# First block of a two-layer Hedgehog/Mish kernel: statistics behind the low weights, one fold chunk between a half's products, the second block's rows counted and normalized ahead of the second queries

## The chip, the cores and the metric

The kernel runs on one core of one Trainium2 chip. A core has five engines that each work through their own instructions in order: TensorE (PE in the profile; its weight loads are PEld), VectorE (DVE), ScalarE (ACT), GpSimd (POOL) and SyncE (SP), which issues the DMA transfers. They wait for each other through semaphores. The metric is the time of one execution on the device in microseconds (us).

## The reference

Two kinds of layer alternate, twice each, on x of 2048 rows by 640 columns, all in 32-bit floats:

```python
def _A_ref(x, wqkv, w_phi, wo):
    B, S, D = x.shape
    H = 32; Dh = D // H
    qkv = (lambda x, *d: x.transpose(*d))((x @ wqkv).reshape(B, S, 3, H, Dh), 2, 0, 3, 1, 4)
    q, k, v = qkv[0], qkv[1], qkv[2]
    pq = jnp.einsum("bhsd,hdf->bhsf", q, w_phi)
    pk = jnp.einsum("bhsd,hdf->bhsf", k, w_phi)
    phi_q = jnp.concatenate([_softmax(pq, axis=-1), _softmax(-pq, axis=-1)], axis=-1)
    phi_k = jnp.concatenate([_softmax(pk, axis=-1), _softmax(-pk, axis=-1)], axis=-1)
    kv = jnp.einsum("bhsf,bhsd->bhfd", phi_k, v)
    z  = jnp.einsum("bhsf->bhf", phi_k)
    num = jnp.einsum("bhqf,bhfd->bhqd", phi_q, kv)
    den = jnp.einsum("bhqf,bhf->bhq", phi_q, z)[..., None] + 1e-6
    o = num / den
    return (lambda x, *d: x.transpose(*d))(o, 0, 2, 1, 3).reshape(B, S, D) @ wo

# _B_ref: dense (w1, b1), Mish, dense (w2)
x = x + _A_ref(_layernorm(x, axis=-1), A_wqkv, A_w_phi, A_wo)
x = x + _B_ref(_layernorm(x, axis=-1), B_w1, B_b1, B_w2)
x = x + _A_ref(_layernorm(x, axis=-1), A_wqkv, A_w_phi, A_wo)
x = x + _B_ref(_layernorm(x, axis=-1), B_w1, B_b1, B_w2)
```

## The kernel before

The 2048 rows are worked in eight blocks of 256, each of two tiles of 128 rows (`NB`, `BT`). Each weight and each normalized, transposed activation is kept as a high part (a copy rounded to the matmul's input type, made on ACT) and a low part (what the rounding left, made on DVE or POOL). A product is then three matmuls: high by high, high activation by low weight, low activation by high weight (`project_half`).

The attention layer has a first half (`attend_first`), which makes the features of queries and keys and the values, sums keys by values into one PSUM bank (`kva`), and sends the query features to DRAM; and a second half (`attend_second`), which reads them back, averages and multiplies by `wo`. The dense layer follows (`dense`).

In the very first layer the query and key weights are first folded with `w_phi`: `fold` multiplies a raw chunk of the transposed weights by the block-diagonal `w_phi` (`bd`, of which `differences` takes one feature per head from the others). For the queries there are five row chunks k of 128 (`KD`) by six column chunks t; t = 0 to 2 make the first half of the query weights (c = 0), t = 3 to 5 the second (c = 1). Each half needs five PSUM banks (`banks_of_five`), one for each k. `query_parts` (L527) splits the folded weights into high (`r2h`) and low (`r2l`). The key weights are folded later in the same way (`fold_keys`, L589) into `r1h` and `r1l`, two banks to a chunk k. The value weights are loaded and split by the generator `v_weights` (L178), one chunk at each `next`: an issue on SP, a copy on ACT, a subtraction here on POOL.

The first block runs by hand: L508 to L622 stand under a manual schedule, in which PE, SP, ACT, DVE and POOL keep the order of the code among these instructions. In other parts of the program the build decides the order of ACT, DVE and POOL, and it may place instructions of those parts between those of the hand-written block; so it does with the DMA issues on SP, too: `spill_qk_weights` (L204) of later blocks, the mask (L626) and the bias (L987) land among the loads of the first. Transfers use eight semaphores in turn (an issue waits for the landing of the transfer eight before it).

The stages of the hand-written block, in the order of PE: 24 transposes of the identity whose result nobody reads (L511), the folds of t = 0 and 1, the transposes of the first tile's rows (`turn`), the folds of t = 2, the first half's fifteen products, the folds of t = 3 to 5, the transposes of the second tile's rows, the second half's fifteen products, the second tile's thirty products, the key folds 0 to 4, the values of both tiles, and then the transposes of the second block's rows and its keys.

`features` (L415) makes query and key features out of a tile's products, in steps that the caller spreads: copies (ACT), two reductions and two subtractions (DVE, one of them on POOL where `pool_sub` is set), the exponential (ACT), a sum and reciprocal (DVE) and a product (POOL).

PSUM tiles `one` are four banks, `mm` two double banks, each handed out again when its readers are done: so the values of tile 1 write the bank that key fold 3's low part has read, and key fold 4 the double bank that fold 0's low parts have read.

Of the kernel before, what the change touches and what calls it, by code (L numbers as in the profile page):

```python
# [10 lines left out]
AF = mybir.ActivationFunctionType  # L11
# [5 lines left out]
P = 128  # L17
# [5 lines left out]
KD = D // P  # L23
KF = F // P
BT = 2
# [4 lines left out]
HC = D // 2  # L30
DF = DH - 1
FC = H * DF // 2
# [5 lines left out]
SKEW = 2  # L38
V_ORDER = (0, 1, 4, 2, 3)
FOLD = (6, 6, 6, 6, 4, 4)  # L40
TURNS = 24
LAYERS = 2
LN_EPS = 1e-5
DEN_EPS = 1e-6
# [7 lines left out]
def kernel(  # L52
# [25 lines left out]
    def one_tile():  # L78
        return psum.tile([P, 512], F32, tag="one", name="one", bufs=4)
# [271 lines left out]
    def row_tile():  # L351
        return work.tile([P, D], F32, tag="xn", name="xn", bufs=4)

    def normed(b, xt):

        xn = [row_tile() for _ in range(BT)]
        for t in range(BT):
            act(xn[t], xt[:, t, :], AF.Identity,
                                 bias=stats[:, b, 1, t:t + 1], scale=stats[:, b, 0, t:t + 1])
        return Transposed(xn)  # L360

    def normalize(b, dst, src):
        for t in range(BT):
# [26 lines left out]
            project_half(ps[c], xts, t, ws, col, c, ks, w=w, final=ks[-1])  # L390
        return ps

    def project_half(ps, xts, t, ws, col, c, ks=range(KD), w=HC, final=KD - 1):
        sl = slice(t * P, (t + 1) * P)
        cs = slice(col + c * w, col + (c + 1) * w)
        for k in ks:
            h, l, wh, wl = xts.hs[k], xts.ls[k], ws[k][0][:, cs], ws[k][1][:, cs]
            for n, (a, r) in enumerate(((h, wh), (h, wl), (l, wh))):
                nc.tensor.matmul(ps[:, :w], a[:, sl], r, start=(k == 0 and n == 0),  # L399
                                 stop=(k == final and n == 2))  # L400

    def both(ps, w=HC):

# [44 lines left out]
    def attend_first(layer, x_src, first):  # L448
# [30 lines left out]

        def queries(xts, i, ps=None):  # L480
            e = query_tile(i)
            yield from features(project(xts, i % BT, q_ws, 0, w=FC) if ps is None else ps, e, True)

            nc.vector.transpose(e, e)  # L484
            b, t = divmod(i, BT)
            dst = e_d[b].rearrange("(j f) (t q s) -> t q f j s", f=32, t=BT, s=32)
            for q in range(4):
                nc.sync.dma_start(dst[t, q], e[32 * q:32 * q + 32].rearrange("f (j s) -> f j s", s=32))
                if b == NB - 1:
                    yield  # L490
# [15 lines left out]
        if first is None:  # L506
            E = mybir.EngineType
            with tc.manual_schedule(engines={E.PE, E.SP, E.Activation, E.DVE, E.Pool}):  # L508
                written[0] = True
                ps = one_tile()  # L510
                for _ in range(TURNS):  # L511
                    nc.tensor.transpose(ps[:, :P], ident, ident)
                xt = x_tile()
                rows = [row_tile() for _ in range(BT)]
                bd = big_tile()[:120, :720].rearrange("p (t c) -> p t c", t=6)

                def fetch_first(t):
                    nc.sync.dma_start(xt[:, t], row_block(x_src, 0)[:, t])

                def normalize_first(t):  # L520
                    act(rows[t], xt[:, t], AF.Identity, bias=stats[:, 0, 1, t:t + 1], scale=stats[:, 0, 0, t:t + 1])

                def banks_of_five():
                    ma, mb = mm_tile(), mm_tile()
                    return [ma[:, 0], ma[:, 1], mb[:, 0], mb[:, 1], one_tile()]

                def query_parts(banks, c, ks):  # L527
                    for n in range(2):
                        for k in ks:
                            fold_parts(q_ws, banks[k], k, c, (n,))  # L530

                fetch_first(0)
                load_phi(bd, False)
                raw = load_raw(0, range(3))
                load_phi(bd, True)
                fetch_first(1)
                raw += load_raw(0, range(3, 6))
                mvs = [norm_stats(0, xt)]
                differences(bd, 120, slice(0, 3), 120)
                norm_scale(0, mvs, 0)  # L540
                normalize_first(0)
                differences(bd, 120, slice(3, 5), 120)
                differences(bd, 80, slice(5, 6), 80)
                q_ws = [r2_pair(k) for k in range(KD)]
                kv_ws = [r1_pair(k) for k in range(KD)]
                xts = FirstRows()
                banks = banks_of_five()
                for t in range(2):
                    for k in range(KD):
                        fold(banks[k], bd, raw, k, t)  # L550
                turned, last = one_tile(), one_tile()
                xts.turn(0, rows[0], turned, last[:, :P])
                for k in range(KD):
                    fold(banks[k], bd, raw, k, 2)
                xts.split(0)
                query_parts(banks, 0, (0, 1))
                query_parts(banks, 0, (2, 3))
                query_parts(banks, 0, (4,))
                mvs = [norm_stats(1, xt)]
                norm_scale(0, mvs, 1)  # L560
                pq = [one_tile()]
                project_half(pq[0], xts, 0, q_ws, 0, 0, w=FC)
                vw = v_weights(kv_ws, nc.gpsimd)
                for _ in range(3):
                    next(vw)
                banks = banks_of_five()
                for k in range(KD):
                    for t in range(3, 6):
                        fold(banks[k], bd, raw, k, t)
                query_parts(banks, 1, (0, 1))  # L570
                normalize_first(1)
                query_parts(banks, 1, (2, 3))
                query_parts(banks, 1, (4,))
                xts.turn(1, rows[1], one_tile(), last[:, P:2 * P])
                xts.split(1)
                pq.append(one_tile())
                project_half(pq[1], xts, 0, q_ws, 0, 1, w=FC)
                next(vw)
                next(vw)
                raw = load_raw(1)  # L580
                g0 = queries(xts, 0, pq)
                next(g0)
                next(g0)
                p1 = project(xts, 1, q_ws, 0, w=FC)
                next(g0)
                g1 = queries(xts, 1, p1)
                next(g1)

                def fold_keys(k):  # L589
                    mm = None if k % 2 else mm_tile()  # L590
                    banks = [one_tile(), one_tile()] if k % 2 else [mm[:, 0], mm[:, 1]]
                    for t in range(6):
                        fold(banks[t // 3], bd, raw, k, t)
                    return lambda n: [fold_parts(kv_ws, banks[c], k, c, (n,)) for c in range(2)]

                parts = [fold_keys(k) for k in range(4)]
                parts[0](0)
                next(g1)
                parts[1](0)
                parts[0](1)  # L600
                next(g1)
                parts[1](1)
                parts[2](0)
                parts[3](0)
                next(g0)
                parts[2](1)
                parts[3](1)
                parts.append(fold_keys(4))
                parts[4](0)
                vs = [v_tile() for _ in range(BT)]  # L610
                xt = fetch(x_src, 1)
                mvs = [norm_stats(t, xt) for t in range(BT)]
                norm_scale(1, mvs)
                ready = last_scale[0]
                v = [values(xts, t, vs[t]) for t in range(BT)]
                next(v[0])
                next(g1)
                parts[4](1)
                nxt = normed(1, xt)
                kva = one_tile()  # L620
                nc.vector.memset(kva[:, :360], 0.0)
                next(v[1])  # L622
            written[0] = False
            with tc.manual_schedule(engines={E.PE, E.SP}):
                pending += [g0, g1]
                nc.sync.dma_start(mask, bass.AP(tensor=head_mask.tensor, offset=head_mask.offset,  # L626
                                                ap=[[1, 120], [21 * 120, 3], [1, 1]]))
                nxt.step()
                nxt.step()
                for t in range(BT):  # L630
                    g = keys(xts, t, vs[t])
                    next(g)
                    if t == 0:
                        nxt.step()
                    advance()
                    pending.append(g)
        else:
            nxt, kv_ws = first
            load_k_weights(kv_ws)
            q_ws = load_q_weights()  # L640
# [422 lines left out]
```

## Time and profile before

| | |
|---|---|
| median of 3 runs | 1363.98 us |
| lowest, highest | 1363.42, 1364.98 us |
| profiled execution, its own time | 1363.75 us |
| its span, first to last instruction | 1362.0 us |
| instructions | 30917 |
| bytes read from HBM, written | 104.61 MB, 62.59 MB |

The span is cut into 40 equal slices on the page; the first two of them, some 68 us, hold the work around the change. A digit is the busy share in tenths:

```profile
PE   9999999999999999999999999999999999999998
DVE  5988788877787887778778988878768776676775
DMA  9614324798614542334472434459974231233200
```

What is to be read there: PE is busy at nine tenths or more in nearly every slice; in the first slice the DMA engines are full and DVE is half idle, and in the second DVE is full. The rows of the timeline give start and duration in us, engine, line, operation, what is written from what, and in brackets the idle time before the instruction with what ended it.

### The profile page before, as it was taken

How to read it: one execution, taken by the hardware profiler on the slowest of the kernel's cores; microseconds unless marked ns; L12 is line 12 of the kernel's file. 1: busy time of each engine (PE TensorE's matmuls, PEld its weight loads, DVE VectorE, ACT ScalarE, POOL GpSimd, SP SyncE). 2: the span in 40 equal slices, each digit the busy share in tenths (PEclk: the TensorE clock that was granted, in tenths of full speed). 3: DMA queues.
4: the chain of work that ended last, by engine and by line, in shares of the span. 5: the costliest groups of instructions: out<-in, count | busy, mean ns of one | idle time of the engine just before them, and what ended most of it. 6: DMA issues, size and time to landing. Idle time of an engine off the chain costs nothing.

```text
span 1362.0 us, 30917 instructions
## 1 busy us (share of the span) xinstructions
PE 1349.2 (99%) x12890; PEld 1337.6 (98%) x12890; DVE 1063.8 (78%) x1805; ACT 584.5 (43%) x1039; POOL 471.0 (35%) x361
## 2 busy tenths in 40 slices
PE   9999999999999999999999999999999999999998
PEld 8999999999999999999999999989999999999998
DVE  5988788877787887778778988878768776676775
ACT  5443444322454545445444344432236444444443
POOL 3345644434222222222216556744341211111111
PEclk9999999999999999999999999999999999999999
DMA  9614324798614542334472434459974231233200
GB/s 343 175 41 76 80 41 86 224 283 304 190 39 96 117 117 72 61 101 111 135 241 56 82 71 78 79 144 278 278 256 130 78 79 30 88 97 98 76 22 20
DMA packets 350613, 169.21 MB, mean 124 GB/s; under 512 B 287225, under 2 KB 323817, under 8 KB 350473
## 3 DMA queue, kind: packets, MB, share of 16 engines
q1 hardware_dynamic: 350473, 167.23, 45.8%
q8 instruction: 101, 1.65, 0.5%
q14 instruction: 39, 0.32, 0.1%
HBM read 104.61 MB, written 62.59 MB: 123 GB/s over the span
## 4 chain that ended last, share of the span: by engine, by line
PE 93%; DMA 2%; DVE 2%; POOL 1%; ACT 0%; issue 0%; SPq 0%; DVEq 0%; POOLq 0%; ACTq 0%
PE mm L399 26%; PE one L859 25%; PE mm L901 24%; PE one L399 12%; PE mm L753 3%; PE one L311 2%; PE one L475 2%; DMA big<-e_d 1%; DMA v<-in_wv 1%; DVE r L484 0%; DVE r L438 0%; DMA big<-in_phi_bd 0%; POOL r L440 0%; POOL big L440 0%; DVE m L429 0%
## 5 line engine op out<-in xcount | busy, mean ns | idle before, releaser
L901 PE MATMUL mm<-r2h,ol 128*128 128x320 f32 x1280 | 304.9, 309 | 0.0
L885 POOL TENSOR_TENSOR ol<-big,ol 128x512 fp32r<-128x512 f32 (+1 forms) x98 | 129.4, 1321 | 486.8 <-ACT ol L884 402.8
L859 PE MATMUL one<-xtl,r1h 128*128 128x256 f32 x960 | 268.2, 279 | 0.0
L859 PE MATMUL one<-xth,r1l 128*128 128x256 f32 x960 | 268.0, 279 | 0.0
L859 PE MATMUL one<-xth,r1h 128*128 128x256 f32 x960 | 265.9, 279 | 0.0
L901 PEld LDWEIGHTS mm<-r2h,ol 128*128 128x128 f32 x1280 | 219.2, 188 | 0.0
L901 PE MATMUL mm<-r2l,ol 128*128 128x320 f32 x640 | 197.3, 309 | 0.0
L399 PE MATMUL mm<-r1h,xth 128*128 128x304 f32 (+1 forms) x600 | 184.9, 308 | 0.0
L399 PE MATMUL mm<-r1l,xth 128*128 128x304 f32 (+1 forms) x600 | 183.7, 306 | 0.0
L399 PE MATMUL mm<-r1h,xtl 128*128 128x304 f32 (+1 forms) x600 | 183.5, 306 | 0.0
L859 PEld LDWEIGHTS one<-xtl,r1h 128*128 128x128 f32 x960 | 180.4, 188 | 0.0
L859 PEld LDWEIGHTS one<-xth,r1l 128*128 128x128 f32 x960 | 180.4, 188 | 0.0
L859 PEld LDWEIGHTS one<-xth,r1h 128*128 128x128 f32 x960 | 179.6, 188 | 0.0
L874 DVE TENSOR_SCALAR big<-big 128x512 f32<-128x512 f32 (+1 forms) x98 | 56.6, 578 | 111.5 <-ACT big L872 111.3
L440 POOL TENSOR_TENSOR big<-big,r 128x1280 f32<-128x1280 f32 x42 | 101.1, 2410 | 64.9 <-DVE r L439 38.9
L872 ACT ACTIVATE big<-one,b1s 128x256 f32<-128x256 f32 x192 | 80.9, 468 | 93.3 <-PE one L859 92.5
L901 PEld LDWEIGHTS mm<-r2l,ol 128*128 128x128 f32 x640 | 120.2, 188 | 0.0
L876 ACT ACTIVATE big<-big,two 128x512 f32<-128x512 f32 (+1 forms) x98 | 70.1, 716 | 115.7 <-DVE big L875 115.6
L884 ACT ACTIVATE ol<-big 128x512 fp32r<-128x512 f32 (+1 forms) x98 | 60.9, 622 | 133.4 <-DVE big L883 133.3
L399 PEld LDWEIGHTS mm<-r1h,xth 128*128 128x128 f32 x600 | 112.8, 188 | 0.6
L399 PEld LDWEIGHTS mm<-r1h,xtl 128*128 128x128 f32 x600 | 112.7, 188 | 0.3
L399 PEld LDWEIGHTS mm<-r1l,xth 128*128 128x128 f32 x600 | 112.8, 188 | 0.1
(154 smaller groups left out, 3118.5 us busy)
## 6 DMA issues: line engine op xcount, KB each, us to landing
big<-e_d SPq DMA_DIRECT2D x32, 640.0 KB, 7.7
x_d<-xt SPq DMA_DIRECT2D x23, 640.0 KB, 4.1
e_d<-r SPq DMA_DIRECT2D x88, 160.0 KB, 4.0
xt<-x_d SPq DMA_DIRECT2D x22, 640.0 KB, 5.4
n_d<-xn SPq DMA_DIRECT2D x176, 80.0 KB, 2.2
xt<-in_x SPq DMA_DIRECT2D x15, 640.0 KB, 4.2
xn<-x_d SPq DMA_DIRECT2D x28, 320.0 KB, 4.6
v<-n_d SPq DMA_DIRECT2D x30, 256.0 KB, 3.1
```

The costliest lines, as they stand in the source:

```text
L311: nc.tensor.transpose(ps[:, c, t * P:(t + 1) * P], self.rows[t][:, (c0 + c) * P:(c0 + c + 1) * P], ident)
L399: nc.tensor.matmul(ps[:, :w], a[:, sl], r, start=(k == 0 and n == 0), stop=(k == final and n == 2))
L440: nc.gpsimd.tensor_tensor(eg, eg, r.unsqueeze(2).to_broadcast([P, 2 * H, DH]), op=ALU.mult)
L475: nc.tensor.matmul(kva[32 * q:32 * q + DH + 1, c:c + 2 * DH], v[:, (DH + 1) * h:(DH + 1) * (h + 1)], e[:, 2 * DH * h:2 * DH * (h + 1)], st ...
L753: nc.tensor.matmul(po[64 * q:64 * q + 64, c, GW * j:GW * j + w], phs[g][:n, s0:s0 + 64], kvb[:n, g, :w], start=True, stop=True)
L859: nc.tensor.matmul(ph[:, j, :], l, r, start=(n == 0), stop=(n == 3 * KD - 1))
L872: exps[0] = nc.scalar.activation(part(ta, 0)[:, j - js.start], ph[:, j, :], AF.Exp, bias=b1s[:, 2 * pr + j:2 * pr + j + 1]).ins
L874: nc.vector.tensor_scalar_min(e, e, E_CAP)
L876: nc.scalar.activation(r, n, AF.Ln, bias=two)
L884: nc.scalar.activation(ah[:, js], n, AF.Copy)
L885: nc.gpsimd.tensor_tensor(al[:, js], n, ah[:, js].bitcast(F32), op=ALU.subtract)
L901: nc.tensor.matmul(pys[t][:, c, :HC], l[:, j, sl], r, start=(f == 0 and n == 0), stop=(f == KF - 1 and n == 2))
```

## The change

All of it is in the first block of the first layer, but for one argument that also holds in the second layer. L numbers are those of before.

- `TURNS`: 18 transposes of the identity in place of 24.
- `differences` of the first three column chunks now come ahead of the first tile's statistics (`norm_stats`) on DVE.
- `banks_of_five` hands out the single bank first and then the two double banks.
- Each half's products are ordered anew: for all five chunks high by high and low by high (`ns=(0, 2)`), then for all five high by low (`ns=(1,)`). Between the two parts of the first half stand the second half's folds of chunk k = 0.
- `query_parts` takes the chunks as (0), (1, 2), (3, 4) in the first half and (0), (1, 2), (3, 4) in the second, the second tile's normalization between (0) and (1, 2).
- `next(vw)`: one chunk of value weights ahead of the second half's folds in place of three, one ahead of the second half's products, three behind the first tile's first feature step.
- `pool_sub` of the queries is `i >= BT`: the first subtraction of the first two tiles of a layer is made on DVE.
- The second block's fetch, statistics and scales come ahead of the low parts of the key folds, its normalization (`normed_rows`, split off from `normed`) ahead of the second tile's exponential; the low parts of the key folds and the feature steps of the two tiles stand in another order.

```diff
-TURNS = 24
+TURNS = 18
...
+    def normed_rows(b, xt):
+
+        xn = [row_tile() for _ in range(BT)]
+        normalize(b, xn, [xt[:, t, :] for t in range(BT)])
+        return xn
+
     def normed(b, xt):
-
-        xn = [row_tile() for _ in range(BT)]
-        for t in range(BT):
-            act(xn[t], xt[:, t, :], AF.Identity,
-                                 bias=stats[:, b, 1, t:t + 1], scale=stats[:, b, 0, t:t + 1])
-        return Transposed(xn)
+        return Transposed(normed_rows(b, xt))
...
-    def project_half(ps, xts, t, ws, col, c, ks=range(KD), w=HC, final=KD - 1):
+    def project_half(ps, xts, t, ws, col, c, ks=range(KD), w=HC, final=KD - 1, ns=(0, 1, 2), end=2):
         sl = slice(t * P, (t + 1) * P)
         cs = slice(col + c * w, col + (c + 1) * w)
         for k in ks:
             h, l, wh, wl = xts.hs[k], xts.ls[k], ws[k][0][:, cs], ws[k][1][:, cs]
-            for n, (a, r) in enumerate(((h, wh), (h, wl), (l, wh))):
+            for n in ns:
+                a, r = ((h, wh), (h, wl), (l, wh))[n]
                 nc.tensor.matmul(ps[:, :w], a[:, sl], r, start=(k == 0 and n == 0),
-                                 stop=(k == final and n == 2))
+                                 stop=(k == final and n == end))
...
-            yield from features(project(xts, i % BT, q_ws, 0, w=FC) if ps is None else ps, e, True)
+            yield from features(project(xts, i % BT, q_ws, 0, w=FC) if ps is None else ps, e, i >= BT)
...
-                    return [ma[:, 0], ma[:, 1], mb[:, 0], mb[:, 1], one_tile()]
+                    return [one_tile(), ma[:, 0], ma[:, 1], mb[:, 0], mb[:, 1]]
...
+                differences(bd, 120, slice(0, 3), 120)
                 mvs = [norm_stats(0, xt)]
-                differences(bd, 120, slice(0, 3), 120)
...
-                query_parts(banks, 0, (0, 1))
-                query_parts(banks, 0, (2, 3))
-                query_parts(banks, 0, (4,))
+                for ks in ((0,), (1, 2), (3, 4)):
+                    query_parts(banks, 0, ks)
                 mvs = [norm_stats(1, xt)]
                 norm_scale(0, mvs, 1)
                 pq = [one_tile()]
-                project_half(pq[0], xts, 0, q_ws, 0, 0, w=FC)
+                project_half(pq[0], xts, 0, q_ws, 0, 0, w=FC, ns=(0, 2), end=None)
                 vw = v_weights(kv_ws, nc.gpsimd)
+                next(vw)
+                banks = banks_of_five()
+                for t in range(3, 6):
+                    fold(banks[0], bd, raw, 0, t)
+                query_parts(banks, 1, (0,))
+                project_half(pq[0], xts, 0, q_ws, 0, 0, w=FC, ns=(1,), end=1)
+                for k in range(1, KD):
+                    for t in range(3, 6):
+                        fold(banks[k], bd, raw, k, t)
+                normalize_first(1)
+                query_parts(banks, 1, (1, 2))
+                query_parts(banks, 1, (3, 4))
+                xts.turn(1, rows[1], one_tile(), last[:, P:2 * P])
+                xts.split(1)
+                next(vw)
+                pq.append(one_tile())
+                project_half(pq[1], xts, 0, q_ws, 0, 1, w=FC, ns=(0, 2), end=None)
+                project_half(pq[1], xts, 0, q_ws, 0, 1, w=FC, ns=(1,), end=1)
+                g0 = queries(xts, 0, pq)
+                next(g0)
                 for _ in range(3):
                     next(vw)
-                banks = banks_of_five()
-                for k in range(KD):
-                    for t in range(3, 6):
-                        fold(banks[k], bd, raw, k, t)
-                query_parts(banks, 1, (0, 1))
-                normalize_first(1)
-                query_parts(banks, 1, (2, 3))
-                query_parts(banks, 1, (4,))
-                xts.turn(1, rows[1], one_tile(), last[:, P:2 * P])
-                xts.split(1)
-                pq.append(one_tile())
-                project_half(pq[1], xts, 0, q_ws, 0, 1, w=FC)
-                next(vw)
-                next(vw)
                 raw = load_raw(1)
-                g0 = queries(xts, 0, pq)
-                next(g0)
                 next(g0)
                 p1 = project(xts, 1, q_ws, 0, w=FC)
                 next(g0)
...
                 parts = [fold_keys(k) for k in range(4)]
-                parts[0](0)
-                next(g1)
-                parts[1](0)
-                parts[0](1)
-                next(g1)
-                parts[1](1)
-                parts[2](0)
-                parts[3](0)
-                next(g0)
-                parts[2](1)
-                parts[3](1)
-                parts.append(fold_keys(4))
-                parts[4](0)
                 vs = [v_tile() for _ in range(BT)]
                 xt = fetch(x_src, 1)
                 mvs = [norm_stats(t, xt) for t in range(BT)]
+                for k in range(2):
+                    for n in range(2):
+                        parts[k](n)
                 norm_scale(1, mvs)
                 ready = last_scale[0]
+                next(g1)
+                parts[2](0)
+                parts[3](0)
+                parts[2](1)
+                parts[3](1)
+                nxt_rows = normed_rows(1, xt)
+                next(g1)
+                next(g0)
+                parts.append(fold_keys(4))
+                parts[4](0)
+                parts[4](1)
                 v = [values(xts, t, vs[t]) for t in range(BT)]
                 next(v[0])
                 next(g1)
-                parts[4](1)
-                nxt = normed(1, xt)
+                nxt = Transposed(nxt_rows)
                 kva = one_tile()
                 nc.vector.memset(kva[:, :360], 0.0)
                 next(v[1])
```

## The prediction

> **What bounds the kernel now.** First the page: the share of busy time. Then, since the change touches only the first some 45 us, the waits of TensorE (PE) in the first 110 us.
>
> ```profile
> PE 1349.2 (99%) x12890; PEld 1337.6 (98%) x12890; DVE 1063.8 (78%) x1805; ACT 584.5 (43%) x1039; POOL 471.0 (35%) x361
> PE one L512 <- POOL ident masks.py:199: 1.3, 1, 1.3
> PE one L399 <- DVE r2l L273: 1.2, 2, 0.7
> PE mm L262 <- DVE r1l L273: 0.6, 1, 0.6
> ```
>
> PE is the bound. In those 110 us it waits 3.1 us, of which 1.3 are the start that nobody touches. The change can win the other 1.8, and what PE does too slowly or needlessly before its first product. Where that lies is in PE's timeline (start, duration):
>
> ```profile
> 1.35 5.38 PE L512 MATMUL one<-ident 128*128 128x128 f32 x24 [1.35 <-POOL ident masks.py:199]
> 6.52 1.48 PE L262 MATMUL mm<-big,raw 120*128 120x114 f32 x8
> 9.18 0.71 PE L339 MATMUL one<-ident,xn 128*128 128x128 f32 x5
> 11.05 0.40 PE L399 MATMUL one<-r2h,xth 128*128 128x304 f32 x1
> 11.95 0.41 PE L399 MATMUL one<-r2l,xth 128*128 128x304 f32 x1 [0.49 <-DVE r2l L273]
> 14.02 0.56 PE L262 MATMUL mm<-big,raw 120*128 120x114 f32 x4
> 18.76 0.41 PE L399 MATMUL one<-r2h,xth 128*128 128x304 f32 x1 [0.73 <-DVE r2l L273]
> 20.96 0.30 PE L399 MATMUL mm<-r2h,xth 128*128 128x304 f32 x1
> 25.16 1.23 PE L262 MATMUL mm<-big,raw 120*128 120x114 f32 x10
> 31.24 1.31 PE L262 MATMUL mm<-big,raw 120*128 120x114 f32 x10 [0.60 <-DVE r1l L273]
> 32.58 0.39 PE L399 MATMUL one<-r1h,xth 128*128 128x320 f32 x1
> 37.06 0.30 PE L399 MATMUL one<-r1h,xth 128*128 128x320 f32 x1
> ```
>
> The stages: 24 idle transposes (1.35), folds of chunks 0 to 2, first half's 15 products (11.05), folds of chunks 3 to 5 (14.02), second half's products (18.76), the second tile's 30 products (20.96), key folds 0 to 3 (25.16), key fold 4 (31.24), values of tile 0 (32.58) and of tile 1 (37.06). From there PE has no wait up to 110 us, so a lead at 37.06 is a lead at the end.
>
> **Part 1: six transposes fewer, differences ahead of the statistics.** 24 transposes take 6.52 - 1.35 = 5.17, 0.215 each; 18 end at 5.2. The first fold then needs its differences and its raw rows:
>
> ```profile
> big<-in_phi_bd SPq DMA_DIRECT2D x1, 168.8 KB, 3.4
> raw<-in_wqk_t SPq DMA_DIRECT2D x1, 320.0 KB, 4.1
> 1.68 1.30 SPq L236 DMA_DIRECT2D raw<-in_wqk_t  x3
> 3.94 0.89 DVE L279 BATCH_NORM_STATS2 bn<-xt 128x6 f32<-128x320 f32 x2 [3.05 <-DMA xt<-in_x]
> 4.98 0.60 DVE L255 TENSOR_TENSOR big<-big 120x114 f32<-120x114 f32 x3
> 6.37 0.92 ACT L124 ACTIVATE xn<-xt,stats 128x640 f32<-128x640 f32 x1 [4.37 <-DVE stats L292]
> ```
>
> Raw rows land at 1.68 + 4.1 = 5.8; the differences can start when phi lands (issued just before, 4.6) and end at 5.2. So folds start at 5.85 instead of 6.52. The statistics slip from 3.94 to 5.2 and with them the normalized rows, which come 6.37 - 3.94 = 2.43 later, at 7.6, done 8.5. PE wants them after two folds, at 8.8 (the folds took 2.7; some of them run at the slow spacing, below). The slip is covered with 0.3 to spare; PE is 0.4 ahead at the first product, 10.65.
>
> **Part 2: products by high weights first, one fold chunk, then by low weights.** The instructions are the same 15 products and 15 folds, in another order.
>
> ```profile
> 10.52 1.52 ACT L271 ACTIVATE r2h<-mm 128x342 fp32r<-128x342 f32 x4
> 11.38 1.78 DVE L273 TENSOR_TENSOR r2l<-mm,r2h 128x342 fp32r<-128x342 f32 x4
> 13.49 0.88 DVE L279 BATCH_NORM_STATS2 bn<-xt 128x6 f32<-128x320 f32 x2
> 16.07 0.92 ACT L124 ACTIVATE xn<-xt,stats 128x640 f32<-128x640 f32 x1
> ```
>
> High parts come each 0.36 (1.52/4) on ACT, low ones each 0.44 on DVE, last low one at 13.3 instead of 13.5. The ten high products go with ACT to 12.4, the chunk (0.67 by the five chunks that fill 14.02 to 17.3) ends at 13.1, the low ones at 13.6: there PE had reached 14.02 with the chunk still to do, so the lead is 0.4 + 0.67 = 1.1. The other four chunks end at 16.3. The second tile's rows follow the statistics by 16.07 - 13.49 = 2.6, so 15.9 to 16.8, with the four remaining second-half copies behind them on ACT (16.8 + 4 x 0.36 = 18.2). The high products keep pace with them, the low ones follow the last low part (18.7): the half ends at about 19 instead of 20.96. Tile 1's 30 products take 25.16 - 20.96 = 4.2 and end at 23.2 instead of 25.16. Lead: 2.
>
> **Part 3: the loads, moved behind a wait on SP.** The built program's order on SP is what the diff does not show: after the first value-weight load come the mask, the bias and a spill of `r2h` of chunk 0 (L207), and only behind it the other four value-weight loads, the key weights' six raw loads and the second block's x. That spill waits for chunk 0's second-half copy on ACT.
>
> ```profile
> 12.85 1.56 ACT L138 ACTIVATE r1h<-xn 128x640 fp32r<-128x640 f32 x2 [0.46 <-DMA xn<-in_wv]
> 7.99 0.86 SPq L137 DMA_DIRECT2D xn<-in_wv  x2
> wp_d<-r1l SPq DMA_DIRECT2D x1, 304.0 KB, 2.4
> xt<-in_x SPq DMA_DIRECT2D x1, 320.0 KB, 3.2
> GB/s 343 175 41 76 80 41 86 224 283 304 190 39 96 117 117 72 61 101 111 135 241 56 82 71 78 79 144 278 278 256 130 78 79 30 88 97 98 76 22 20
> 12.83:17.79 4.96, 4.96 (x45) 4.96 (x43) 2.94 (x9) 4.49 (x9) 3.00 (x4) 1.00 1.05 399
> 17.80:23.10 5.30, 4.57 (x34) 4.34 (x32) 3.14 (x8) 3.09 (x9) 5.30 (x4) 1.00 1.06 317
> ```
>
> ACT copies value weights at 12.85 when they land (0.74), then chunk 0's second half (0.38): the spill goes out at 14.0, where before the loads behind it went out from 8 us on. Up to and with the second block's x the queue then holds 304 + 4x320 + 5x320 + 200 + 640 = 4024 KB, 4.12 MB. At the 399 GB/s of the full queue that is 10.3 us, and a lone 304 KB spill landed after 2.4, 1.6 more than its share: x lands at 14.0 + 1.6 + 10.3 = 25.9. The bounds: 3.2 after issue for a lone 320 KB and the 317 GB/s of the stretch in which mask and bias moved give 29.4; full overlap of the latency gives 24.3. I take 25.9: mask and bias now move in the pause. The last raw chunk lands 1.64 ahead of x, at 24.2; key fold 0 reaches it at 23.2 + 1.1 = 24.3. Just in time: from there each later microsecond of loading is one of PE.
>
> **Part 4: VectorE ahead of the values.** DVE now stands, in order: tile 0's reductions and both subtractions (one was GpSimd's), second block's statistics, low parts of key folds 0 and 1, tile 1's reductions, third block's statistics, two subtractions, low parts of folds 2 and 3. Values of tile 1 write the PSUM bank that fold 3's low part frees.
>
> ```profile
> 21.77 1.54 DVE L429 TENSOR_REDUCE m<-r 128x32 f32<-128x640 f32 x2 [2.16 <-ACT r L124]
> 23.10 1.28 POOL L430 TENSOR_TENSOR r<-r,m 128x640 f32<-128x640 f32 x1
> 52.81 0.82 DVE L430 TENSOR_TENSOR big<-big,m 128x640 f32<-128x640 f32 x1
> 30.25 0.85 DVE L273 TENSOR_TENSOR r1l<-mm,r1h 128x342 fp32r<-128x342 f32 x2
> 41.34 1.66 DVE L279 BATCH_NORM_STATS2 bn<-xt 128x6 f32<-128x320 f32 x4
> 36.13 0.21 DVE L281 BATCH_NORM_AGGREGATE mv<-bn 128x2 f32<-128x12 f32 x1
> 39.69 0.34 DVE L292 TENSOR_SCALAR stats<-mv,stats 128x1 f32<-128x1 f32 x2 [1.09 <-POOL stats L290]
> ```
>
> Tile 0's reductions start 0.8 after the half's products, as before (21.77 - 20.96), and with 1.54 + 2 x 0.82 its part ends at 23; then DVE, and everything behind it, waits for x until 25.9. From there: statistics 2.1 (1.66 and two aggregates), folds 0 and 1 1.6, scales 0.3, reductions 1.5, third block 1.6, subtractions 0.82 x 2 and aggregates 0.2, folds 2 and 3 1.6: 10.5, to 36.4. PE: key folds 0 to 3 take 5.5 without a wait (25.16 to 31.24 less 0.6), to 28.7; fold 4 needs fold 0's low part, 28.9, so that wait is nearly gone; values of tile 0 start 1.34 later, at 30.2, take 37.06 - 32.58 = 4.48 and end at 34.7. Values of tile 1 could follow, 2.3 ahead of before, and wait 1.7 us for DVE instead: 0.7 of the lead is left. Set out instruction by instruction, with starts that overlap the end before by the 0.08 that the rows show, it is 1.1. I take **0.85**.
>
> Hidden: the two early normalizations (0.9 each) fill an idle ACT; GpSimd loses 2 x 1.28. In the second layer, too, the first two tiles' subtractions move, 1.64 us more on DVE, while PE waits for no DVE there.
>
> **Sum.** Profiled execution 1363.75 (span 1362.0 and 1.8 around it), less 0.85: 1362.9. The median of the runs shown is 1363.98, 0.2 above it.
>
> **Rivals.** (a) *The lead is kept whole:* if loads land 1.5 us earlier than worked out, DVE is done before PE asks and 2.3 to 2.4 are won: 1361.4. For it: the 24.3 of the bound. Against: the queue's order is fixed.
>
> (b) *The clock stays low.* Spacing on PE was 0.215 up to the first folds and about 0.11 later (L339: five in 0.71). Now PE stands idle from 5.2 to 5.85, in the middle of that change. If the gap starts a wait anew, some 20 fold passes before the first product cost 0.105 more each, 2.1, and the spill and the loads behind it move along: result between 1363.2 and 1365.0. For it: the change came only after 5.9 us of unbroken work. Against: the gap is short. The Trainium skill (TensorE: Matmul & The Clock Gate, Part 1) says that about 3.4 us of sustained work release the clock, in a free-running window; by that rule an unlucky window gives this case. Its Part 4 says that transposes do not count as such work; the trace disagrees, for the spacing fell about 1 us after the last of the 24.
>
> (c) *Slower: the pause on SP decides.* One mechanism: the loads behind the spill come late and hold key folds and DVE. It costs PE one to one, and the kernel is slower than before once x lands after 26.8. At the 343 GB/s of the page's first slice (4.12 MB: 12.0 us) x lands at 27.6 and the time is 1364.6; at the far bound 1366.4. For it: before, these loads were out five us sooner and the queue was never empty. Against: 399 GB/s held wherever only large rows moved.
>
> (d) *It does not do what it says:* the low parts already came in time, so products end where they did. The waits of 0.49 and 0.73 speak against it; time unchanged, 1363.8.
>
> **How the numbers follow.** Forecast 0.45, (a) 0.2, (b) 0.13, (c) 0.17, (d) 0.05. What 0.2% is (2.7 us) can just be told from no change. Faster than 1361.3 needs the best of (a) and a bit: 0.13. Slower than 1366.7 needs the far end of (c) or (c) with (b): 0.1. Within: 0.77. The range, 1361.2 to 1365.2, takes in (a) and the nearer part of (b) and (c); the forecast's own is 1362.4 to 1363.4.
>
> **What would show it.** Right: the spill on SP at about 14, x of block 1 landing near 26, a wait of PE of 1 to 2 us on DVE's `r1l` at the values, none at 31. Wrong: waits of the key folds for `raw` (c), fold spacing of 0.2 after 8 us (b), no wait at the values (a).

## The result: slower, and the profile after

| kernel | median | lowest to highest | executions |
|---|---|---|---|
| before | 1363.01 us | 1361.54 to 1364.98 us | 8 |
| after | 1370.66 us | 1365.53 to 1374.14 us | 8 |

The ratio is 1.0053, with an interval of 1.0042 to 1.0063: slower by half a per cent, and outside the range of the prediction (1361.2 to 1365.2). The profiled execution of after took 1374.14 us (span 1372.4), 10.4 us more than that of before. The eight executions of after have mean granted clocks of 0.992 to 0.999: the one at 0.999 took 1365.53 us, the seven at 0.992 to 0.996 took 1368.17 us or more.

First, of after, the page's row of the granted clock in 40 slices, and the waits of PE in the first 110 us (in all, times, longest):

```profile
PEclk9899999999999999999999999999999999999999
```

```profile
PE mm L262 <- DMA raw<-in_wqk_t: 2.3, 5, 0.9
...
PE one L262 <- DMA raw<-in_wqk_t: 0.8, 1, 0.8
PE mm L262 <- DMA xn<-in_wqk_t: 0.4, 1, 0.4
```

The waits on VectorE that bounded the kernel before (1.2 and 0.6 us) are gone; in their place the key folds wait 2.7 us for raw rows (2.3 and 0.4). That is 0.9 us more than the two waits that went, and little beside 10.4. The 0.8 us ahead of the first folds is the pause that the prediction puts between 5.2 and 5.85. The second digit of the clock's row, 8, is the clue to the rest. Next SP's queue in after (start, duration), then PE at the key folds:

```profile
7.98 0.33 SPq L137 DMA_DIRECT2D xn<-in_wv  x1
...
14.26 0.33 SPq L207 DMA_DIRECT2D wp_d<-r2h  x1
...
16.64 2.81 SPq L236 DMA_DIRECT2D raw<-in_wqk_t  x5
19.55 0.65 SPq L236 DMA_DIRECT2D xn<-in_wqk_t  x1
21.58 1.21 SPq L447 DMA_DIRECT2D xt<-in_x  x2
```

```profile
5.92 0.45 PE L262 MATMUL one<-big,raw 120*128 120x114 f32 x2 [0.85 <-DMA raw<-in_wqk_t]
...
10.22 0.41 PE L401 MATMUL one<-r2h,xth 128*128 128x304 f32 x1
...
23.34 0.45 PE L262 MATMUL mm<-big,raw 120*128 120x114 f32 x2 [0.15 <-DMA raw<-in_wqk_t]
...
25.14 0.48 PE L262 MATMUL mm<-big,raw 120*128 120x114 f32 x2 [0.59 <-DMA raw<-in_wqk_t]
26.52 0.48 PE L262 MATMUL mm<-big,raw 120*128 120x114 f32 x2 [0.91 <-DMA raw<-in_wqk_t]
...
28.50 2.34 PE L262 MATMUL one<-big,raw 120*128 120x114 f32 x10
```

The spill goes out at 14.26, as predicted (14.0), and PE reaches key fold 0 at 23.2 (23.34 less the wait), as predicted. But the fold takes from 23.3 to 28.5 in place of 1.3 us, and the next one's ten passes take 2.34 us where before they took 1.23 to 1.31: no wait stands there, every pass is slower. The windows show why. They are cut at the edges of the clock's records, 3.41 us apart; the columns are the stretch, its length, the busy time of PE, PEld, DVE, ACT and POOL with counts, the granted clock, the DMA share and GB/s:

```profile
21.61:25.02 3.41, 2.50 (x16) 1.92 (x14) 2.99 (x2) 1.75 (x3) 2.84 (x3) 1.00 1.06 388
25.02:28.43 3.41, 1.64 (x8) 1.13 (x9) 0.00 (x0) 1.69 (x3) 1.01 (x1) 1.00 1.02 331
28.43:31.84 3.41, 3.41 (x18) 3.41 (x18) 2.27 (x7) 1.59 (x4) 0.33 (x2) 0.50 1.02 402
...
922.72:926.14 3.42, 1.67 (x52) 1.44 (x46) 2.57 (x8) 0.00 (x0) 0.00 (x0) 1.00 1.05 382
926.14:929.55 3.41, 2.45 (x29) 2.37 (x30) 0.75 (x4) 0.00 (x0) 0.00 (x0) 0.50 1.04 362
```

In the stretch of the waits PE is busy for 1.64 of 3.41 us (48%), and from its end the granted clock is 0.50 for four stretches, 28.43 to 42.09 or 13.65 us, in which PE is busy throughout. The same happens once more at 926 us, behind a stretch with 1.67 us of work, for 6.83 us.

What each part costs in this execution can be read from the distance between the same instruction in both profiles. Rows of before, then of after:

```profile
26.46 1.28 PE L262 MATMUL one<-big,raw 120*128 120x114 f32 x10
...
41.46 1.25 PE L311 MATMUL one<-ident,xn 128*128 128x128 f32 x8
...
919.31 0.80 PE L753 MATMUL mm<-kvb,big 120*64 120x63 f32 x20 [1.40 <-DMA big<-e_d]
```

```profile
49.10 1.03 PE L311 MATMUL one<-ident,xn 128*128 128x128 f32 x8
...
927.10 1.33 PE L758 MATMUL mm<-kvb,big 120*64 120x63 f32 x20 [2.28 <-DMA big<-e_d]
```

At key fold 0 after is 1.8 us ahead (23.34 against 25.16), at key fold 1 it is 2.0 behind (28.50 against 26.46): the late rows cost 3.8 us, more than the 2.7 of the waits, because the passes between them stand alone, some 0.45 us for two, where ten in a row took 1.28. At the transposes of the second block's rows it is 7.6 behind: the half clock cost 5.6 more. At 927 us the distance is 7.8, of which 0.9 is a longer wait for `big<-e_d`, and at the end it is 10.4: the second half clock cost 2.6. So the clock took 8.2 us and the late rows 3.8, less what after was ahead. Whether the second drop belongs to the change is not shown.

### The profile page after: what moved, and what is told of

Its sections match the earlier page's. It is cut to its first block, busy times and chain, and to the rows that moved or that the text cites. A ratio compares the mean times of both kernels' runs of the same rounds, so it can differ in the third digit from the quotient of the medians.

```text
span 1372.4 us, 30908 instructions
## 1 busy us (share of the span) xinstructions
PE 1357.6 (99%) x12884; PEld 1344.9 (98%) x12884; DVE 1068.0 (78%) x1809; ACT 585.0 (43%) x1039; POOL 467.3 (34%) x357
## 4 chain that ended last, share of the span: by engine, by line
PE 94%; DMA 3%; DVE 2%; POOL 1%; SPq 0%; issue 0%; ACT 0%; DVEq 0%; POOLq 0%
PE mm L401 26%; PE one L864 25%; PE mm L906 24%; PE one L401 12%; PE mm L758 3%; PE one L311 2%; PE one L477 2%; DMA big<-e_d 1%; DMA xn<-in_wqk_t 1%; DMA v<-in_wv 0%; DVE r L486 0%; PE mm L262 0%; DVE r L440 0%; DMA raw<-in_wqk_t 0%; DMA xn<-in_wv 0%; PE one L262 0%
```

## Experiments

All ratios are to the kernel before, run beside each.

**1. The spill behind the loads.** The changed kernel, with SP's spills of the first block (`spill_qk_weights`) issued only behind the second block's x (`loads_out` is that transfer). The order on PE, ACT and POOL is that of after.

```diff
...
-                spill_qk_weights(kv_ws, q_ws, b - 1)
+                with tc.issue_after(loads_out):
+                    spill_qk_weights(kv_ws, q_ws, b - 1)
```

> The changed kernel, with one DMA issue moved: the spill of the query weights (L207 of before) stands on SP behind the first block's loads and x of the next blocks, not ahead of four value-weight and six key-weight loads. Nothing else differs on PE, ACT or POOL. Theory 1 (the loads behind the spill come late, PE waits for them at the key folds, and the idle lets the granted clock fall to half): no wait of PE for raw loads, no half clock between 20 and 50 us, time 1361 to 1363, about 1 under before. Rival A (the new order of products, low parts and subtractions itself costs): key folds wait no more, but the time stays above 1366.

Measured: 1362.75 us (1361.21 to 1367.5), ratio 0.9998 (0.9988 to 1.0007), mean clock 0.998 to 1.0 in every execution. The loss is gone once no spill stands ahead of the loads; in after it was one. The gain is not shown either: in this profile the clock rises only at 10.1 us (7.4 in before, 4.5 in after), and the values of tile 1 start at 37.11 (before: 37.06). The records of the clock begin with its rise, so the mean clock does not count the slow start. Nor does it tell everything: one execution here took 1367.5 us at a mean clock of 0.999, and why is open.

**2. PE filled where it waits.** The changed kernel with its late loads, and five idle transposes ahead of each but the first column chunk of key fold 0, into columns of the same banks that nobody reads.

```diff
+FILL = 5
...
                     for t in range(6):
+                        for _ in range(FILL if k == 0 and t else 0):
+                            nc.tensor.transpose(banks[t // 3][:, 384:512], ident, ident)
                         fold(banks[t // 3], bd, raw, k, t)
```

> The changed kernel, loads as late as there, with 25 transposes of the identity (0.109 us each, 2.7 us in all) into unused columns of key fold 0's banks, five ahead of each fold of t = 1 to 5, so that PE is busy while it waits. Nothing reads them. Theory 1 (most of the loss is the clock that falls after PE's idle time, not the wait itself): granted clock 1.0 from 20 to 50 us, time 1363 to 1366. Rival B (the lateness itself is the loss; the clock follows something else): half clock again from about 28 us, or a time above 1368 with the clock held.

Measured: 1366.18 us (1364.52 to 1368.57), ratio 1.0020 (1.0011 to 1.0028), mean clock 0.999 to 1.0 in every execution. The waits of PE and the stretch with the fill, in its profile:

```profile
PE one L402 <- DVE r1l L274: 1.1, 1, 1.1
PE mm L263 <- DMA raw<-in_wqk_t: 0.5, 2, 0.2
```

```profile
24.26:27.67 3.41, 2.96 (x25) 2.47 (x24) 0.76 (x1) 1.99 (x3) 2.17 (x2) 1.00 1.06 292
27.67:31.08 3.41, 3.41 (x32) 3.30 (x30) 1.60 (x5) 1.55 (x4) 0.19 (x1) 1.00 1.01 404
```

Work that computes nothing makes the kernel 4.5 us faster than after (1.0053 less 1.0020, times 1363), with the raw rows as late as there (the last chunk lands at 27.95 us, in after at 28.15): that part is the clock. The time is 0.2 us above the range of the theory, whose clock came as expected. The 2.9 us that stay above before (1366.18 less the 1363.31 beside it) are put down to the lateness itself, seen as key folds that wait for rows or stand behind the fill, and as the wait on `r1l`.

**3. The spill alone, in the old order.** The kernel before, with the spill of `r2h`, chunk 0, on SP ahead of four value-weight loads and the raw key loads. With these loads the splitting of their weights on ACT and GpSimd comes later too, as in the change; PE's order is that of before.

```diff
-            nc.sync.dma_start(wp_d[0, s, k], q_ws[k][s][:, :FW].bitcast(F32))
+            if s or k:
+                nc.sync.dma_start(wp_d[0, s, k], q_ws[k][s][:, :FW].bitcast(F32))
...
+                nc.sync.dma_start(wp_d[0, 0, 0], q_ws[0][0][:, :FW].bitcast(F32))
+                staged = {}
+                for k in V_ORDER[1:]:
+                    staged[k] = (row_tile, row_tile, v_tile, v_tile, big_tile)[k]()[:, :D]
+                    nc.sync.dma_start(staged[k], wv[k * P:(k + 1) * P, :])
```

> The kernel before, with PE's, DVE's (up to three rows far later) and POOL's order unchanged: one spill of query weights is issued ahead of the four later value-weight loads and the key-weight loads, as in the changed kernel; the copies of these value weights on ACT stand where the changed kernel has them. Theory 1: the spill goes out at about 16 us, key folds wait 3 to 4 us in all for raw loads, the clock falls to half for 6.8 or 13.7 us: 1368 to 1376. Rival A (the new order of PE's and DVE's work is the cause): 1362 to 1364.5, as before.

Measured: 1370.92 us (1370.41 to 1371.44), ratio 1.0055 (1.0042 to 1.0068), clock 0.994 to 0.996: as much as the whole change costs. The same picture in its windows, two thin stretches and then half the clock for three:

```profile
24.27:27.69 3.42, 2.13 (x13) 1.59 (x12) 0.00 (x0) 0.35 (x1) 3.42 (x3) 1.00 1.05 356
27.69:31.10 3.41, 2.58 (x19) 2.25 (x19) 0.82 (x1) 2.00 (x4) 0.46 (x1) 1.00 1.01 384
31.10:34.51 3.41, 3.41 (x19) 3.41 (x17) 2.73 (x5) 1.54 (x5) 1.27 (x1) 0.50 1.05 408
```

**4. The products alone.** The kernel before with the order of the products and of the banks of the change, and nothing else of it.

> The kernel before with the order of products alone: high weights, one fold chunk, low weights, single bank first; 24 transposes, statistics, loads, subtractions as before. Theory 1 (this part gains what it takes out of PE's waits): 0.5 to 1.5 less than before, 1361.5 to 1362.7, with the waits of 0.49 and 0.73 us for low parts gone. Rival A (this order costs): 1364 or more.

Measured: 1367.2 us (1363.65 to 1370.2), ratio 1.0027 (1.0017 to 1.0037), clock 0.994 to 1.0: a miss for the theory. In this build two spills had again moved ahead of loads, of the last raw chunk and of x (x issued at 21.24, landed at 27.16), and in the profiled execution the clock was at half from 7.8 to 11.2 us, behind a wait of 1.9 us for the first raw rows. Two causes were mixed, so the next run separates them.

**5. The products alone, loads first.** As run 4, with the spills held behind x as in run 1; the code of PE, ACT, DVE and POOL as in run 4.

> The kernel of before with nothing of the change but the order of the products (high weights, one fold chunk, low weights) and of the banks; unlike in the run with the products alone, SyncE keeps before's order, with the spills behind the second block's x. Theory (the loss of the products alone came from the two spills that the build set ahead of the last raw chunk and of x): the order of the products itself costs nothing and gives PE a lead of 1 to 2 us at the key folds, 1361.3 to 1363.0, mean granted clock 0.999 or more in every run. Rival (the order itself breaks up PE's work between 11 and 18 us and sets the clock down): 1364 to 1368, with clocks of 0.994 to 0.998 in some of the runs.

Measured: 1368.1 us (1366.12 to 1368.47), ratio 1.0032 (1.0020 to 1.0044), clock 0.996 to 1.0: the rival's numbers. A wait of its PE, one of its ScalarE, and its windows:

```profile
PE one L401 <- ACT r2h L272: 1.5, 2, 0.9
```

```profile
11.79 0.80 ACT L272 ACTIVATE r2h<-mm 128x342 fp32r<-128x342 f32 x2 [0.99 <-DVE r2l L274]
```

```profile
11.59:15.00 3.41, 2.13 (x14) 1.83 (x15) 2.36 (x6) 2.55 (x6) 0.00 (x0) 1.00 1.02 357
15.00:18.42 3.42, 3.42 (x18) 3.42 (x17) 0.81 (x4) 0.87 (x2) 2.95 (x4) 0.50 1.05 408
```

In the new order of banks the chunks 1 and 2 lie in one double bank, 3 and 4 in the other, while `query_parts` here still takes the chunks as (0, 1), (2, 3), (4). ScalarE's high part of chunk 2 waits 0.99 us for VectorE's low part of chunk 1. PE, behind it, waits 1.5 us in two pieces, is 62% busy in that stretch, and pays three stretches at half clock. That is not the whole loss: the one execution with a mean clock of 1.0 still took 1366.12 us. In after, with the groups (0), (1, 2), (3, 4), neither wait is there. That the shared bank makes the wait is read from the names alone; that the order of the products costs 0.3% without the rest of the change is measured.

**6. Those waits filled.** Run 5 with 13 idle transposes at the two waits.

```diff
...
+                for ks, fill in (((0, 1), 8), ((2, 3), 5), ((4,), 0)):
+                    project_half(pq[0], xts, 0, q_ws, 0, 0, ks=ks, w=FC, ns=(0, 2), end=None)
+                    for _ in range(fill):
+                        nc.tensor.transpose(banks[0][:, 384:512], ident, ident)
```

> The kernel of before with only the products' order changed and the loads in before's order, and 13 idle transposes more on PE: eight behind the first two chunks of the first half's high products and five behind the next two, where PE waited 0.90 and 0.57 us for ScalarE's r2h. They write a part of a free bank that nobody reads. Theory (the run without them lost by the clock, set to half for 10.2 us behind a stretch of 3.41 us in which PE was 62% busy): clock 0.999 or more in every run, 10.2/2 = 5.1 us less than without them, 1361.8 to 1363.6. Rival (the order of the products itself costs the time, by what is late behind it): 1365.5 to 1368.

Measured: 1366.86 us (1363.89 to 1369.3), ratio 1.0027 (1.0017 to 1.0037), clock 0.996 to 1.0: a time in the rival's range, and no gain over run 5 that the intervals show. The drop at 15 us is gone (PE is busy for 3.33 us of 10.59 to 14.00), but others stand later in the profiled execution:

```profile
31.07:34.48 3.41, 2.24 (x20) 2.12 (x19) 3.41 (x6) 2.58 (x6) 0.00 (x0) 1.00 0.99 374
34.48:37.89 3.41, 3.41 (x15) 3.41 (x14) 3.34 (x10) 0.61 (x2) 2.36 (x1) 0.50 1.03 330
```

PE comes to key fold 4 early, waits 1.2 us there for VectorE's `r1l`, is 66% busy in that stretch, and the clock is at half in the next. Nor is the clock all: five executions with a mean clock of 0.999 or 1.0 took 1363.89 to 1366.86 us. That the lead of the products has no use while VectorE's order is the old one fits this; it is not shown by itself.

**7. 24 transposes, spill behind the loads.** Run 1 with `TURNS = 24`.

> The changed kernel with the spills behind the second block's x, as in the run that put the spill behind, and 24 idle transposes in place of 18. Theory (with 18 transposes PE stands still for about 0.5 us just before the first folds, the clock rises at 10.1 us in place of 7.4, and the folds until then take about twice as long): clock up by 7.5 us, PE 1 to 2 us earlier at the key folds than with 18, 1360.8 to 1362.3. Rival (six transposes fewer are worth the 0.65 us they take less and the rise of the clock is chance): 1362.8 to 1363.6, no better than with 18.

Measured: 1362.19 us (1360.98 to 1363.02), ratio 0.9990 (0.9981 to 0.9998), clock 0.999 to 1.0. This version is faster than before, by 0.1%, and also than after (1370.66). Its PE, and VectorE behind x:

```profile
23.21 1.23 PE L263 MATMUL mm<-big,raw 120*128 120x114 f32 x10
...
26.78 0.48 PE L263 MATMUL mm<-big,raw 120*128 120x114 f32 x2 [0.78 <-ACT r L125]
...
35.59 0.41 PE L402 MATMUL one<-r1h,xth 128*128 128x320 f32 x1
```

```profile
22.74 2.06 DVE L435 TENSOR_TENSOR r<-m,r 128x640 f32<-128x640 f32 x1
25.24 0.89 DVE L280 BATCH_NORM_STATS2 bn<-xt 128x6 f32<-128x320 f32 x2 [0.44 <-DMA xt<-in_x]
...
34.69 0.84 DVE L274 TENSOR_TENSOR r1l<-one,r1h 128x342 fp32r<-128x342 f32 x2
```

Key fold 0 starts at 23.21, the values of tile 1 at 35.59, 1.5 ahead of before. The clock rose at 5.2 us here. But run 1's interval overlaps this one's, so that 24 transposes are better than 18 is not shown.

**8. The subtraction back on GpSimd.** Run 7 with `pool_sub` as before the change.

```diff
-            yield from features(project(xts, i % BT, q_ws, 0, w=FC) if ps is None else ps, e, i >= BT)
+            yield from features(project(xts, i % BT, q_ws, 0, w=FC) if ps is None else ps, e, True)
```

> As the run with 24 transposes and the spills behind x, but the first subtraction of the first two tiles of each layer is GpSimd's again, as before the change. Theory (with x in time VectorE has room, and the values of tile 1 do not wait for the key weights' low parts): within 0.5 us of the run with 24 transposes. Rival (VectorE still sets when key fold 4 and the values start): 0.5 to 1.6 us faster than it, for the two subtractions of 0.8 us that leave VectorE.

Measured: 1368.99 us (1367.14 to 1370.25), ratio 1.0039 (1.0027 to 1.0051), clock 0.994 to 0.997: both theories missed, in sign. GpSimd, PE's wait, ScalarE and PE's window there:

```profile
22.18 3.06 POOL L140 TENSOR_TENSOR r1l<-v,r1h 128x640 fp32r<-128x640 f32 x2
25.19 1.27 POOL L433 TENSOR_TENSOR r<-r,m 128x640 f32<-128x640 f32 x1
```

```profile
PE mm L263 <- ACT r L125: 2.9, 1, 2.9
```

```profile
27.41 1.27 ACT L125 ACTIVATE r<-r 128x1280 f32<-128x1280 f32 x1 [5.60 <-DVE r L435]
```

```profile
25.76:29.17 3.41, 0.67 (x7) 0.52 (x5) 2.61 (x7) 1.76 (x3) 0.89 (x2) 1.00 1.04 407
29.17:32.59 3.42, 3.29 (x15) 3.29 (x16) 2.75 (x9) 1.86 (x8) 0.89 (x2) 0.50 1.04 401
```

On GpSimd the subtraction stands behind the value weights' low parts and starts at 25.19. VectorE's second subtraction (L435) follows it, ScalarE's exponential of tile 0 waits for that one, the copies of tile 1 stand behind that on ScalarE, and they hold the double bank that key fold 2 writes: PE waits 2.9 us, is 20% busy, and has half the clock for 10.2 us after. Without the move to VectorE the rest of the order loses 6.8 us (1368.99 against 1362.19).

## Why the prediction was wrong, by its own steps

**Part 1** held for the folds: 5.92 (5.85 predicted). That the first product came at 10.22 in place of 10.65 is the clock, which rose at 4.5 us in after and at 7.4 in before; nothing in the prediction foresaw it.

**Part 2** held in the whole change: PE at key fold 0 at 23.2 in after and in run 7, as predicted. (The 0.36 for a high part is a slip: 1.52/4 is 0.38; over four copies that is 0.1 us. The 0.4 us by which the first product was early are gone by the end of the low products, at 13.5; 13.6 was predicted.) It left out what the order rests on: with the old groups of `query_parts` the high products wait for ScalarE (run 5).

**Part 3** failed, and it is the step that turned the result. The pause was seen and placed right, and so was the traffic behind it (4.12 MB). The size was wrong: x landed at 29.48, not at 25.9, and the last raw chunk at 28.15, not at 24.2. VectorE's first row behind x, and the transfers of after between 15.0 and 29.5 us, when x was in:

```profile
29.50 0.89 DVE L279 BATCH_NORM_STATS2 bn<-xt 128x6 f32<-128x320 f32 x2 [4.87 <-DMA xt<-in_x]
```

```profile
DMA packets 1912, 4.97 MB, mean 343 GB/s; under 512 B 210, under 2 KB 210, under 8 KB 1912
```

At 343 GB/s, 4.12 MB take 12.0 us (27.0); the 0.85 MB that moved besides, of transfers that stand behind x on SP, take 2.5 more. The sum of the prediction had no such traffic. I had taken 399, the rate of one stretch of before, and put the 317 of its neighbour down to mask and bias. In after these had landed before the pause, and the rate still fell under 260 GB/s twice (259 and 248 from 18 to 20 us, 241 from 25 to 26). What makes these dips was not tried.

**Rival (c)** then had the right mechanism and, at its far bound, the right place (x at 29.4, 1366.4 us). Its sign came: waits of the key folds for `raw`. Run 2, in which the clock doesn't fall, measured 1366.18; that it is so near is in part luck, for its idle transposes stand in PE's way too. What the price lacked is the clock: "one to one" was wrong. The late rows, 3.8 us, were followed by four stretches at half clock, 5.6 us more, and in this execution by 2.6 at 926 us; between the medians the clock is 4.5 (run 2 against after). Rival (b) had thought of the clock, but only at the start, and in after it rose early, at 4.5 us. In run 1 that rival came true: the clock rose at 10.1, and the same order reached key fold 0 at 24.73, 1.5 us later than in run 7. The Trainium skill (TensorE: Matmul & The Clock Gate, Part 1, "HAM oscillation") warns of idle gaps longer than about 3.4 us; in after no gap of PE in this place was longer than 0.91, and the clock fell all the same. The measurement decides: several short gaps that left PE 48% busy in one stretch were enough. The Trainium skill (the same page, Part 1, "What's actually happening") gives 3413 ns for the window; the lengths of half clock here agree (13.65 us is four, 6.83 is two).

**Part 4** held where x is in time: in run 7 x lets VectorE start at 25.24, and the last low part of fold 3 ends at 35.53, 10.3 later (10.5 predicted), just as the values of tile 1 start. That PE doesn't wait there is because it had lost 0.78 us at key fold 2, which waits for ScalarE's copies of tile 1; the prediction has no such wait. With x late and PE at full clock (run 2) the wait on `r1l` is there, 1.1 us. The two subtractions took 1.43 and 2.06 there in place of 0.82 each, beside GpSimd's low parts; the wait for x (0.44 left in run 7) covers it. "Hidden" was too little said of GpSimd's relief: run 8 shows that the order needs it.

**The sum**, 0.85 us faster, is near what runs without the spill ahead of the loads show, but that is luck in part. Run 7 has 0.89 (1363.08 beside it, less 1362.19), with 24 transposes and with x at 25.2, for which the prediction's own working gives 1.5, the lead that its profile shows. Run 1, with the change's own 18 transposes, has 0.56, with an interval that holds none. "A lead at 37.06 is a lead at the end" held within 0.6 us in both (1.5 ahead there and 1.6 in the span in run 7, 0.05 behind and 0.5 ahead in run 1), but not in after, 7.6 behind at 49 us and 10.4 at the end.

## What to carry to other kernels

Look at what the build has put between loads on a shared issue queue: a single store that waits for a computed tile holds every load behind it, and run 3 shows that this alone can cost more than the reordering gains. Price a wait of TensorE not by its length but by the stretch of 3.41 us that it falls into: where PE is about half idle there, add, as an estimate, some 2 to 7 us for the clock (one to four stretches at half speed, as seen here). If the wait can't go, filling it with idle transposes won 4.5 us in run 2; in run 6 it won nothing that the intervals show.

## What the runs showed of the hardware

Cut at the clock's own edges, and without the last three stretches of a program, the ten profiles hold five stretches in which PE was busy under half the time at full clock (20, 44, 45, 48 and 49%), and behind all five the granted clock fell to 0.50. At the program's end one stretch with 1.55 of 3.41 us of work was not followed by a fall (run 4, from 1359.48 us), so this is no fixed rule. Between 51 and 82% it fell behind three (62, 66, 75%) and not behind some forty, the lowest of them at 51 and 59%. So the busy share of one stretch doesn't settle it alone; what else counts stays open. The half clock lasted one stretch (runs 4 and 6), two, three (runs 3, 5, 8) or four, though PE was busy for nearly all of it in most of them; why it differs stays open too.

VectorE's subtraction of 128x640 took 1.42 and 2.09 us in after while GpSimd ran subtractions of its own, against 0.82 in the row of before. The rows of after, VectorE and then GpSimd:

```profile
21.09 1.42 DVE L432 TENSOR_TENSOR r<-r,m 128x640 f32<-128x640 f32 x1
22.55 2.09 DVE L434 TENSOR_TENSOR r<-m,r 128x640 f32<-128x640 f32 x1
```

```profile
22.40 3.63 POOL L139 TENSOR_TENSOR r1l<-v,r1h 128x640 fp32r<-128x640 f32 x2 [0.57 <-ACT r1h L138]
```
